# A one-core forward and backward pass of attention and SwiGLU: W' stored untransposed in the second MLP chunk and turned by its load, four q tiles stored earlier, and half of the MLP gradient loads moved to ScalarE's queue

## The chip, the core and the metric

One core of a Trainium2 chip. TensorE (PE) multiplies matrices; VectorE (DVE), ScalarE (ACT) and GpSimd (POOL) do the rest; SyncE (SP), ACT and POOL issue DMAs, which 16 DMA engines carry out. Each issuer has a queue of its own (q1 for SP, q10 for ACT and q0 for POOL in the profile). The metric is the device time of one launch, in microseconds (us), median of several runs.

## What is computed

```python
def _B_ref(x, w1, w3, w2):
    gate = x @ w1;  up = x @ w3
    return (silu(gate) * up) @ w2
def _A_ref(x, wqkv, wo):                    # 32 heads of 20
    q, k, v = heads(x @ wqkv)
    phi = lambda t: where(t > 0, t + 1, exp(t)) + 1e-6
    kv = einsum("hsd,hse->hde", phi(k), v);  z = phi(k).sum(s)
    num = phi(q) @ kv;  den = phi(q) @ z + 1e-6
    return heads_joined(num / den) @ wo
h  = x + _A_ref(layernorm(x), wqkv, wo)
h2 = h + _B_ref(layernorm(h), w1, w3, w2)
# outputs: h2 and, from grad_out, the gradients of x, wqkv, wo, w1, w3, w2
```

(Shortened: the einsums of the reference are written as products, and the reference takes the gradients by differentiation of this function.) S = 2048 rows, D = 640, F = 1728, all in bf16. Rows come in 16 tiles of 128 (t), and in four chunks of 512 (c); F in 13 pieces of 128 and one of 64 (fc); D in five pieces of 128.

## The kernel before

The program's order is written out by hand: each engine runs its instructions in the order in which the Python code records them, with semaphores where one needs another's result. A DMA's completion is a semaphore too. The stages:

1. *Phase 1, to about 75 us.* Layer norm, k, v and the first q tiles; kv is formed without v: the kernel keeps M = phi(k)^T x and applies W_v to it later. phi(q) of tile t, times 1/den, is called r; pqT holds it transposed. r is stored in DRAM as r_d for the backward pass.
2. *The prelude to the MLP, about 75 to 100 us*, the list in `run((...), ...)`. `q_late(t)` forms the last six q tiles; tiles 8 to 15 are not yet divided, and are kept in DRAM (pq_d, by `q_out` and `q_rest`) until `r_load` brings them back in the MLP. `f2_wT(i)` forms 128 rows of the transposed W', where W' = blockdiagonal(kv) wo, in the buffer pkx, and issues a DMA transpose on SP that writes 128 columns of Wp, W' itself. `f2_w_out` stores pkx's part, the transposed W', as wT_d. `f2_half(t, j)` multiplies r by half of Wp, adds x and takes the statistics of the second layer norm; `f2_hn(t)` normalises on DVE and stores hn_d; `f2_ht(t)` turns the tile (on PE with a copy on ACT for the first four, by DMA after them). `mlp_ghh(n)` is one piece of grad_out w2^T.
3. *The MLP, about 100 to 345 us*: for each chunk c and fc, `mlp(c, fc, ...)`. ACT takes sigmoids and copies of two PSUM results, `mlp_pair` has DVE work on two fc at a time, and the results are stored: hh_d by SP, two pieces of gg_d by POOL, where the gate buffer (two of a kind) is free again only when its store has landed. Between the matmuls of fc stand the second product of the chunk before (`o2_steps`), and the attention output and layer norm of the chunk after (`sides`). `r_steps[c]` adds r's work at given fc. At c = 3, fc = 9 wT2, the transposed W', is loaded on SP.
4. *Gradient of w2, 345 to 404 us*, from hh_d.
5. *The backward pass through the MLP's layer norm, 404 to 540 us*: for each tile t, `b_ghn(t)` multiplies a piece of gg_d, loaded by `load_gg(j, c0, c1)` for two tiles at a time into two buffers ggb, with the transposed w1 and w3. `ln_bwd` then gives g_h, the gradient of h; `b_gT(t)` turns it by a DMA transpose on ACT's queue; `b_gr(t)` multiplies it by wT2 two steps later. In the same steps, ACT's queue also turns wo and kvT_d (woT, kvN), 128 rows at a time.
6. *The gradients of wqkv, wo, x, w1 and w3, 540 to 824 us.*

Which queue a DMA stands in, and what stands before it there, is set by the place of its line in this order: `dma` and `dmaT` (a transpose) are SP's, `dmaG` is POOL's, `A.dma_start` and `A.dma_start_transpose` ACT's. An issuing engine waits at a DMA until the data that it needs is there, and all behind it waits too. POOL also takes the power -0.5 of the variances (L154) and some products (L352).

Of the kernel before, what the change touches and what calls it, by code (L numbers as in the profile page):

```python
# [9 lines left out]
P = 128  # L10
BF16 = mybir.dt.bfloat16
# [7 lines left out]
S, D, H, F = 2048, 640, 32, 1728  # L19
DH = D // H  # L20
ST, DT = S // P, D // P
FT, FP = 14, 1792
# [3 lines left out]
NG = 27  # L26
# [29 lines left out]
def kernel(  # L56
# [19 lines left out]
    V, A, T, G, SY = nc.vector, nc.scalar, nc.tensor, nc.gpsimd, nc.sync  # L76
    dma, dmaT, dmaG = SY.dma_start, SY.dma_start_transpose, G.dma_start

    def rows(ap):
        return ap.rearrange("(t p) d -> p t d", p=P)  # L80
# [9 lines left out]
    dram = ctx.enter_context(tc.tile_pool(name="dram", bufs=1, space=bass.MemoryType.DRAM))  # L90
# [2 lines left out]
    pk_d = dram.tile([S, D], BF16, name="pk_d")  # L93
    xn_d = dram.tile([S, D], BF16, name="xn_d")
    m_d = dram.tile([D, D], BF16, name="m_d")
    wT_d = dram.tile([D, D], BF16, name="wT_d")
    kvT_d = dram.tile([D, D], BF16, name="kvT_d")
    dwoT_d = dram.tile([D, D], BF16, name="dwoT_d")
    hn_d = dram.tile([S, D], BF16, name="hn_d")
# [30 lines left out]
    class Stats:  # L130
# [8 lines left out]
        def run(self, src, a, b):  # L139
            for t in range(a, b):  # L140
                for j in range(2):
                    self.part(src, t, j)

        def part(self, src, t, j, mid=None):
            if j == 0:
                self.st[t] = cp.tile([P, 2, 6], F32, name="st6", bufs=4)
            V.bn_stats(out=self.st[t][:, j, :], in_=src[:, t, j * HD:(j + 1) * HD])  # L147
            if j == 0:
                return
            V.bn_aggr(out=self.mv[:, t, :], in_=self.st.pop(t)[:])  # L150
            if mid is not None:
                mid()
            V.tensor_scalar(out=self.ve[:, t:t + 1], in0=self.mv[:, t, 1:2], scalar1=EPS_LN, scalar2=None, op0=ALU.add)
            G.tensor_tensor(out=self.rs[:, t:t + 1], in0=self.ve[:, t:t + 1], in1=mhalf[:, 0:1], op=ALU.pow)  # L154
# [29 lines left out]
    def load_x(a, b):  # L184
        dma(out=x_sb[:, a:b, :], in_=xS[:, a:b, :])
# [35 lines left out]
    def load_g2T(c):  # L221
        g2T[c] = U2.tile([P, DT, W], BF16, name="g2T", tag="g2T", bufs=2)
        dmaT(out=g2T[c][:], in_=goD[c * W:(c + 1) * W, :])
# [87 lines left out]
    pkx = []  # L311
# [332 lines left out]
    def f2_wT(i):  # L644

        acc = [ps.tile([P, 512], F32, name="wt", tag=("o2", "at")[i % 2], bufs=2) for _ in range(2)]
        for c, a, b, bank, off, first in SQ:
            T.matmul(acc[bank][:, off:off + (b - a) * DH], lhsT=wo[:, c, i * P:(i + 1) * P],
                     rhs=bd[:, c, a * DH:b * DH], start=first, stop=True, skip_group_check=True)
        for bank, (a, b) in enumerate(((0, SPLIT_D), (SPLIT_D, H))):  # L650
            (A.copy, V.tensor_copy)[bank](out=pkx[0][:, i, a * DH:b * DH], in_=acc[bank][:, 0:(b - a) * DH])
        dmaT(out=Wp[:, :, i * P:(i + 1) * P], in_=pkx[0][:, i, :])

    def f2_w_out():
        dmaG(out=rows(wT_d), in_=pkx[0][:, 0:DT, :])

    def f2_m_out():
        dmaG(out=m_v[:, 4, :], in_=mbs[:, 0, :])
# [97 lines left out]
    def drain(n):  # L756
        for _ in range(min(n, len(later))):
            later.pop(0)()
# [61 lines left out]
    Wp = U1.tile([P, DT, D], BF16, name="Wp", tag="MW")  # L820
    pkx.append(p1.tile([P, DT + 6, D], BF16, name="pkx", tag="pk"))
    def kv3():
        for m in (2, 3, 4):
            f2_kv(m)

    run((q_late, 10, f2_mT), (q_late, 11, kv3), (phi_rest,), (r_store, 4, 5), (r4_out,),
        (q_late, 12, lambda: (f2_wT(0), f2_wT(1))), (q_late, 13, lambda: (f2_wT(2), f2_wT(3))), (phi_rest,),
        (q_late, 14, lambda: f2_wT(4)), (load_x, 4, 8), (r_head, 5), (r_prod, 7), (r_store, 5, 6), (f2_m_out,),
        (f2_w_out,), (q_out, 8, 10), (q_out, 10, 14), (load_w2T, 8 * P, 10 * P), (mlp_ghh, 4), (q_late, 15),
        (sig_table,), (f2_half, 0, 0), (f2_half, 1, 0), (f2_half, 2, 0), (f2_half, 0, 1), (f2_half, 1, 1), (f2_hn, 0),  # L830
        (f2_half, 2, 1), (f2_hn, 1), (f2_half, 3, 0), (f2_half, 3, 1), (f2_ht, 0), (mlp_ghh, 5), (load_w2T, 10 * P, F),
        (f2_hn, 2), (f2_ht, 1), (mlp_ghh, 6), (r_red, 6), (f2_hn, 3), (f2_ht, 2), (r_inv, 6), (r_scale, 6), (r_T, 6),
        (f2_half, 4, 0), (mlp_ghh, 7), (f2_ht, 3), (f2_half, 4, 1), (r_red, 7), (r_inv, 7), (r_scale, 7), (r_T, 7),
        (r_store, 6, 8))
    p1.release()
    pa = pool("pa", "right")

# [25 lines left out]
    def r_end(t):  # L863
# [4 lines left out]
                13: ((xn_out, 3, dmaG),)},  # L868
               {0: ((r_den, 8),), 1: ((r_end, 8), (r_load, 11)), 2: ((r_den, 9),), 3: ((r_end, 9), (r_load, 12)),
                4: ((r_den, 10), (q_rest,)), 5: ((r_end, 10), (r_load, 13)), 6: ((r_den, 11),),  # L870
                7: ((r_end, 11), (r_load, 14)), 9: ((r_den, 12),), 10: ((r_end, 12), (r_load, 15))},
               {0: ((r_den, 13),), 1: ((r_end, 13),), 3: ((r_den, 14),), 4: ((r_end, 14),), 6: ((r_den, 15),),
                7: ((r_end, 15),)}, {}]
    for c in range(SC):
        hhT[c] = pa.tile([P, FT, W], BF16, name="hhT", bufs=2)
        o2 = o2_steps(c - 1) if c > 0 else None

        def run_side(pos, fc):
            if c + 1 < SC:
                for f, i in sorted(sides[c][pos].get(fc, ()), key=lambda x: (x[0] is f2_ht, x[1])):  # L880
                    f((c + 1) * TPC + i)

        for fc in range(FT):
            mlp(c, fc, lambda: run_side(0, fc))
            drain(1)
            if o2 and not (c == SC - 1 and fc == 5):
                next(o2, None)
            run_side(1, fc)
            drain(1)
            if (c, fc) in ((0, 12), (1, 5)):  # L890
                load_x(8 + 4 * c, 12 + 4 * c)
            if c == 0 and fc in (5, 7, 9, 11):
                a, b = {5: (0, 3), 7: (3, 6), 9: (6, 10), 11: (10, 13)}[fc]
                dma(out=w2[:, a:b, :], in_=B_w2[a * P:b * P, :].rearrange("(c p) n -> p c n", p=P))
                if fc == 11:
                    dma(out=w2[0:FL, FT - 1, :], in_=B_w2[(FT - 1) * P:F, :])
            for f, *t in r_steps[c].get(fc, ()):
                f(*t)
            if c == 2 and fc == 3:
                dmaG(out=rows(kvT_d), in_=bd[:])  # L900
            if fc == (6, 3, 3)[min(c, 2)] and c < SC - 1:
                load_g2T(c + 1)
            if c == SC - 1 and fc == 0:
                g2 = U1.tile([P, ST, D], BF16, name="g2", tag="Q")
                tail = U2.tile([P, DT, P], BF16, name="w13tail", tag="g2T", bufs=2)
            if c == SC - 1 and fc in (1, 2, 5, 6):
                i = (1, 2, 5, 6).index(fc)
                dma(out=g2[:, i * TPC:(i + 1) * TPC, :], in_=goS[:, i * TPC:(i + 1) * TPC, :])
            if c == SC - 1 and fc == 8:
                dma(out=tail[:, :, 0:FL], in_=B_w1[:, F - FL:F].rearrange("(c p) f -> p c f", p=P))  # L910
                dma(out=tail[:, :, FL:P], in_=B_w3[:, 0:P - FL].rearrange("(c p) f -> p c f", p=P))
            if c == SC - 1 and fc == 9:
                wT2 = U1.tile([P, DT, D], BF16, name="wT2", tag="MW")
                dma(out=wT2[:], in_=rows(wT_d))
    drain(1)
    next(o2, None)
    drain(1)
# [34 lines left out]

    ggb = {}

    def load_gg(j, c0, c1):
        if c0 == 0:
            ggb[j] = ba.tile([P, NG, 2 * P], BF16, name="ggb", bufs=2)
        dma(out=ggb[j][:, c0:c1, :],
            in_=gg_d[c0 * P:c1 * P, j * 2 * P:(j + 1) * 2 * P].rearrange("(c p) w -> p c w", p=P))

    def gw2_tail():
# [50 lines left out]
    def b_load(t):  # L1012
        hnb[t] = br.tile([P, D], BF16, name="hnb", bufs=3)
        dma(out=hnb[t][:], in_=hn_v[:, t, :])
        dma(out=r_sb[:, t, :], in_=r_v[:, t, :])
# [40 lines left out]
    def by_dma(t):  # L1056
        return t < ST - 2
# [79 lines left out]
    for t in range(ST):  # L1137
        g = b_ghn(t)

        def part():  # L1140
            next(g, None)

        u = t - 2
        if 2 <= t <= ST - 3:
            load_gg(t // 2 + 1, *((FT, NG) if t % 2 else (0, FT)))
        part()
        part()
        part()
        if t + 2 < ST:
            b_load(t + 2)  # L1150
        if t >= 1:
            ln_rest.pop(t - 1)()
            if by_dma(t - 1):
                b_gT(t - 1)
            if t <= 2 * DT:
                n = (t - 1) % DT
                dst, src = (woT, A_wo) if t <= DT else (kvN, kvT_d)
                A.dma_start_transpose(out=dst[:, :, n * P:(n + 1) * P], in_=src[n * P:(n + 1) * P, :])
        part()
        if u >= 0:  # L1160
            b_gr(u)
        part()
        part()
        if u >= 0:
            b_gq(u)

        if t >= 4:
            load_xn(t - 4, t - 3)
# [290 lines left out]
```

## Time and profile before

| | |
|---|---|
| median of 7 runs | 825.7 us (824.85 to 828.0) |
| the profiled execution | 826.12 us, its span 824.4 us |
| PE busy | 816.3 us, 99% of the span |
| DVE, ACT, POOL busy | 452.8, 319.9, 133.4 us |
| chain of work that ended last | PE 87%, DVE 6%, DMA 4%, issue 1%, ACT 1% |
| DMA, 60 to 120 us | the 16 engines taken 1.00 to 1.12 of the time, 225 to 263 GB/s |
| DMA over the span | 157.58 MB, mean 191 GB/s |

The page gives for each engine its busy time, and for a group of instructions its line, engine, operation, tiles (out<-in) and count. The waits view says who waited for whom: us in total, times, longest. The timeline shows merged instructions in order of time: start, duration, engine, line, operation; the idle time before them stands in brackets with what ended it. In the DMA list stand the issuer, the count, the KB of each and the median us from issue to landing. The trace also holds a record of each DMA packet: queue, start, duration, bytes. Matmuls overlap one another, so a busy PE says only that no gap was seen; the spacing of their starts says more.

### The profile page before, as it was taken

To read this page: it belongs to the slowest core of one execution; us is meant where nothing else is said; L and a number is where in the kernel's file an instruction comes from. 1 tells how busy PE (TensorE), PEld (TensorE's weight loads), DVE (VectorE), ACT (ScalarE), POOL (GpSimd) and SP (SyncE) were. 2 spreads that over 40 slices of the span, in tenths; PEclk is the share of its full clock that TensorE was granted. 3 is DMA by queue.
4 is the path that set the end of the run, shared out by engine and by line. 5 is a ranking of instruction groups with operands and counts; after the bars stand their busy time and mean duration, and the time that the engine had idled before them with its cause. 6 is when DMAs were issued, how large, how long until landed. Compare 5 with 4: busy or idle time off the path is not lost.

```text
span 824.4 us, 14215 instructions
## 1 busy us (share of the span) xinstructions
PE 816.3 (99%) x5549; PEld 522.5 (63%) x5549; DVE 452.8 (55%) x961; ACT 319.9 (39%) x607; POOL 133.4 (16%) x193
## 2 busy tenths in 40 slices
PE   8999999999999999999999999999999999999998
PEld 5677544555555555777777777777777777555554
DVE  7859987999898566300057777772681544200000
ACT  6856787655655666011121212222212334211111
POOL 2244433233322212100001111110220000000000
PEclk9999999999999999999999999999999999999999
DMA  9899999596494555999778899358994788985771
GB/s 242 227 313 224 217 266 293 194 236 172 126 225 127 153 184 167 228 249 262 211 166 182 197 215 197 59 110 179 279 189 108 164 196 183 210 199 128 174 160 38
DMA packets 318338, 157.58 MB, mean 191 GB/s; under 512 B 235456, under 2 KB 311456, under 8 KB 318272
## 3 DMA queue, kind: packets, MB, share of 16 engines
q1 hardware_dynamic: 286256, 120.65, 63.3%
q0 software_dynamic: 7376, 24.81, 9.5%
q10 hardware_dynamic: 24640, 11.23, 6.8%
q8 instruction: 43, 0.70, 0.4%
q14 instruction: 23, 0.19, 0.1%
HBM read 48.15 MB, written 51.46 MB: 121 GB/s over the span
## 4 chain that ended last, share of the span: by engine, by line
PE 87%; DVE 6%; DMA 4%; issue 1%; ACT 1%; POOL 0%; SPq 0%; DVEq 0%; ACTq 0%; POOLq 0%
PE job L1223 19%; PE mm L380 16%; PE ghn L1025 14%; PE gxn L1381 8%; PE o L791 7%; PE gw L980 7%; PE gwo L1110 3%; PE gr L1082 3%; PE dkv L1327 3%; DMA gg_d<-gate 2%; PE macc L411 2%; DVE st L147 2%; PE big L265 2%; PE at L610 1%; PE dkv L1255 1%
## 5 line engine op out<-in xcount | busy, mean ns | idle before, releaser
L1223 PE MATMUL job<-gb,hnN 128*128 128x432 bf16 (+2 forms) x656 | 117.0, 342 | 0.0
L1025 PEld LDWEIGHTS <-ggb 128*128 128x128 bf16 x864 | 84.5, 98 | 32.8
L1223 PEld LDWEIGHTS <-hnN 128*128 128x128 bf16 x656 | 63.6, 98 | 53.4
L380 PE MATMUL mm<-pqT,w 128*128 128x512 bf16 x405 | 93.6, 379 | 0.3 <-ACT pqT L703 0.3
L380 PEld LDWEIGHTS <-w 128*128 128x128 bf16 x540 | 52.5, 98 | 63.4 <-issue 1.3
L1227 ACT CAST obs<-job 128x432 bf16<-128x432 f32 (+3 forms) x61 | 29.3, 481 | 123.0 <-PE job L1223 123.0
L791 PE MATMUL o<-w,hhT 128*128 128x320 bf16 x448 | 67.5, 299 | 0.0
L1025 PE MATMUL ghn<-w13a,ggb 128*128 128x320 bf16 x448 | 63.5, 299 | 0.0
L1025 PE MATMUL ghn<-w13b,ggb 128*128 128x320 bf16 x416 | 61.4, 299 | 0.0
L380 PE MATMUL mm<-g2T,w2T 128*128 128x512 bf16 x240 | 59.6, 379 | 0.3 <-ACT gate L732 0.3
L791 PEld LDWEIGHTS <-hhT 128*128 128x128 bf16 x448 | 43.8, 98 | 23.6
L980 PE MATMUL gw<-g,hb 128*128 128x320 bf16 x416 | 56.8, 299 | 0.0
L1090 POOL TENSOR_TENSOR sz<-Zb,g_h 128x640 f32<-128x640 bf16 x16 | 20.2, 1262 | 199.3 <-DVE g_h L1088 199.3
L980 PEld LDWEIGHTS <-hb 128*128 128x128 bf16 x416 | 40.6, 98 | 16.0 <-issue 0.3
L1381 PE MATMUL gxn<-wqT,gT 128*128 128x320 bf16 x320 | 48.7, 299 | 0.0
L400 ACT CAST ghh<-mm 128x512 bf16<-128x512 f32 x48 | 28.3, 589 | 47.0 <-PE mm L380 41.5
L730 ACT ACTIVATE sig<-mm 128x512 bf16<-128x512 f32 x56 | 33.6, 600 | 26.5 <-PE mm L380 23.6
L265 PE MATMUL big<-wqkv,pqT 128*128 128x320 bf16 x260 | 40.0, 299 | 2.0 <-DMA wqkv<-in_A_wqkv_dram 1.0
L1037 ACT ACTIVATE gs<-ghn 128x640 bf16<-128x640 f32 x16 | 11.3, 704 | 79.0 <-PE ghn L1025 74.0
L380 PEld LDWEIGHTS <-w2T 128*128 128x128 bf16 x260 | 25.3, 98 | 23.8 <-issue 0.6
L265 PEld LDWEIGHTS <-pqT 128*128 128x128 bf16 x320 | 30.4, 98 | 15.3 <-issue 1.6
L1381 PEld LDWEIGHTS <-gT 128*128 128x128 bf16 x320 | 31.3, 98 | 12.2
(207 smaller groups left out, 1280.4 us busy)
## 6 DMA issues: line engine op xcount, KB each, us to landing
gg_d<-gate POOLq DMA_DIRECT2D x24, 256.0 KB, 4.0
hh_d<-hhT SPq DMA_DIRECT2D x24, 256.0 KB, 2.7
gg_d<-ghh POOLq DMA_DIRECT2D x24, 256.0 KB, 3.5
ggb<-gg_d SPq DMA_DIRECT2D x6, 896.0 KB, 5.6
ggb<-gg_d SPq DMA_DIRECT2D x6, 832.0 KB, 7.2
x_sb<-in_A_x_dram SPq DMA_DIRECT2D x7, 640.0 KB, 6.9
out_dram<-obs ACTq DMA_DIRECT2D x39, 108.0 KB, 3.0
ggb<-gg_d SPq DMA_DIRECT2D x2, 1728.0 KB, 12.6
```

Source lines behind the costliest of these rows:

```text
L265: T.matmul(acc, lhsT=pqT[:, c, t * P:(t + 1) * P], rhs=wqkv[:, c, n0:n0 + HD], start=(c == 0), stop=(c == DT - 1))
L380: T.matmul(acc[:], lhsT=w[:, c, fc * P:(fc + 1) * P], rhs=rhs[:, c, :], start=(c == 0), stop=(c == DT - 1))
L400: A.copy(out=ghh[n // 2][:, n % 2, :], in_=acc[:])
L730: A.activation(sig[:, i, :], gp[:], AF.Sigmoid)
L791: T.matmul(o2["ps"][:, 0:HD], lhsT=hhT[c][:, fc, i * P:(i + 1) * P], rhs=w2[:, fc, j * HD:(j + 1) * HD], start=(fc == 0), stop=(fc == FT - 1))
L980: T.matmul(acc[:, j, 0:HD], lhsT=hb[b][:, t, i * P:(i + 1) * P], rhs=g2[:, t, j * HD:(j + 1) * HD], start=(t == 0), stop=(t == ST - 1))
L1025: T.matmul(acc[:, j, 0:HD], lhsT=ggb[t // 2][:, k, lo:lo + P], rhs=rhs[:, j * HD:(j + 1) * HD], start=(k == 0), stop=(k == NG - 1))
L1082: T.matmul(gr[t][:, j, 0:HD], lhsT=ghT[t][:, c, :], rhs=wT2[:, c, j * HD:(j + 1) * HD], start=(c == 0), stop=(c == DT - 1))
L1110: T.matmul(acc[m][:, j, 0:n], lhsT=r_sb[:, t, m * P:(m + 1) * P], rhs=g_hx[:, t, j * HD:j * HD + n], start=(t == 0), stop=(t == ST - 1))
L1223: T.matmul(acc[:, 0:n], lhsT=lhs[:, t, m * P:(m + 1) * P], rhs=rhs(t), start=(t == 0), stop=(t == ST - 1))
L1227: A.copy(out=ob, in_=acc[:, 0:n])
L1381: T.matmul(acc[:, j, 0:HD], lhsT=g, rhs=wqT[:, k, j * HD:(j + 1) * HD], start=(k == 0), stop=(k == 14))
```

## The change

- `f2_w_out` is gone from the prelude. In its place `w_out` stores Wp, W' untransposed, as w_d on POOL's queue, in chunk 1 after fc = 11. wT2's load at c = 3, fc = 9 becomes a DMA transpose of w_d on SP.
- `q_out(8, 10)` and a new `q_out(10, 12)` stand before `q_late(12)`; `q_out(12, 14)` stays at the old place.
- `load_x(4, 8)` becomes `load_x(4, 6)` there, and `load_x(6, 8)` near the end of the list, between `f2_half(4, 1)` and `r_red(7)`.
- `f2_hn(2)` stands before `f2_half(3, 1)` instead of after `mlp_ghh(5)` and `load_w2T(10 P, F)`.
- In stage 5 the first half of a ggb load (14 of 27 pieces) stays on SP at the even step t. The second (13 pieces), which stood on SP at the head of the odd step, is issued by ACT in the even step, after g_h's transpose and that of wo or kvT_d. The number of loads and their bytes are the same.

```diff
-    wT_d = dram.tile([D, D], BF16, name="wT_d")
+    w_d = dram.tile([D, D], BF16, name="w_d")
...
-    def f2_w_out():
-        dmaG(out=rows(wT_d), in_=pkx[0][:, 0:DT, :])
+    def w_out():
+        dmaG(out=rows(w_d), in_=Wp[:])
...
-    run((q_late, 10, f2_mT), (q_late, 11, kv3), (phi_rest,), (r_store, 4, 5), (r4_out,),
-        (q_late, 12, lambda: (f2_wT(0), f2_wT(1))), (q_late, 13, lambda: (f2_wT(2), f2_wT(3))), (phi_rest,),
-        (q_late, 14, lambda: f2_wT(4)), (load_x, 4, 8), (r_head, 5), (r_prod, 7), (r_store, 5, 6), (f2_m_out,),
-        (f2_w_out,), (q_out, 8, 10), (q_out, 10, 14), (load_w2T, 8 * P, 10 * P), (mlp_ghh, 4), (q_late, 15),
-        (sig_table,), (f2_half, 0, 0), (f2_half, 1, 0), (f2_half, 2, 0), (f2_half, 0, 1), (f2_half, 1, 1), (f2_hn, 0),
-        (f2_half, 2, 1), (f2_hn, 1), (f2_half, 3, 0), (f2_half, 3, 1), (f2_ht, 0), (mlp_ghh, 5), (load_w2T, 10 * P, F),
-        (f2_hn, 2), (f2_ht, 1), (mlp_ghh, 6), (r_red, 6), (f2_hn, 3), (f2_ht, 2), (r_inv, 6), (r_scale, 6), (r_T, 6),
-        (f2_half, 4, 0), (mlp_ghh, 7), (f2_ht, 3), (f2_half, 4, 1), (r_red, 7), (r_inv, 7), (r_scale, 7), (r_T, 7),
-        (r_store, 6, 8))
+    run((q_late, 10, f2_mT), (q_late, 11, kv3), (phi_rest,), (r_store, 4, 5), (r4_out,), (q_out, 8, 10),
+        (q_out, 10, 12), (q_late, 12, lambda: (f2_wT(0), f2_wT(1))), (q_late, 13, lambda: (f2_wT(2), f2_wT(3))),
+        (phi_rest,), (q_late, 14, lambda: f2_wT(4)), (load_x, 4, 6), (r_head, 5), (r_prod, 7), (r_store, 5, 6),
+        (f2_m_out,), (q_out, 12, 14), (load_w2T, 8 * P, 10 * P), (mlp_ghh, 4), (q_late, 15), (sig_table,),
+        (f2_half, 0, 0), (f2_half, 1, 0), (f2_half, 2, 0), (f2_half, 0, 1), (f2_half, 1, 1), (f2_hn, 0),
+        (f2_half, 2, 1), (f2_hn, 1), (f2_half, 3, 0), (f2_hn, 2), (f2_half, 3, 1), (f2_ht, 0), (mlp_ghh, 5),
+        (load_w2T, 10 * P, F), (f2_ht, 1), (mlp_ghh, 6), (r_red, 6), (f2_hn, 3), (f2_ht, 2), (r_inv, 6), (r_scale, 6),
+        (r_T, 6), (f2_half, 4, 0), (mlp_ghh, 7), (f2_ht, 3), (f2_half, 4, 1), (load_x, 6, 8), (r_red, 7), (r_inv, 7),
+        (r_scale, 7), (r_T, 7), (r_store, 6, 8))
...
-                7: ((r_end, 11), (r_load, 14)), 9: ((r_den, 12),), 10: ((r_end, 12), (r_load, 15))},
+                7: ((r_end, 11), (r_load, 14)), 9: ((r_den, 12),), 10: ((r_end, 12), (r_load, 15)), 11: ((w_out,),)},
...
-                dma(out=wT2[:], in_=rows(wT_d))
+                dmaT(out=wT2[:], in_=w_d[:, :])
...
-    def load_gg(j, c0, c1):
+    def load_gg(j, c0, c1, q=dma):
         if c0 == 0:
             ggb[j] = ba.tile([P, NG, 2 * P], BF16, name="ggb", bufs=2)
-        dma(out=ggb[j][:, c0:c1, :],
+        q(out=ggb[j][:, c0:c1, :],
...
-        if 2 <= t <= ST - 3:
-            load_gg(t // 2 + 1, *((FT, NG) if t % 2 else (0, FT)))
+        ahead = 2 <= t <= ST - 4 and t % 2 == 0
+        if ahead:
+            load_gg(t // 2 + 1, 0, FT)
...
                 A.dma_start_transpose(out=dst[:, :, n * P:(n + 1) * P], in_=src[n * P:(n + 1) * P, :])
+            if ahead:
+                load_gg(t // 2 + 1, FT, NG, A.dma_start)
```

## The prediction

> **What bounds the kernel now.** I read the busy table first, then the waits of TensorE (PE), the chain, and then the four places that they name, engine by engine. The busy table:
>
> ```profile
> span 824.4 us, 14215 instructions
> ...
> PE 816.3 (99%) x5549; PEld 522.5 (63%) x5549; DVE 452.8 (55%) x961; ACT 319.9 (39%) x607; POOL 133.4 (16%) x193
> ```
>
> PE is busy for all but 8.1 us. PE's instruction order is the same in both kernels, so no PE work can be saved; the change can only shorten or lengthen PE's gaps. Asked for 75 to 345 us, all that lies between phase 1 and the weight gradients, the waits of PE are:
>
> ```profile
> PE mm L380 <- ACT pqT L703: 0.3, 1, 0.3
> PE mm L380 <- ACT gate L732: 0.3, 1, 0.3
> PE at L610 <- DMA Wp<-pkx: 0.2, 1, 0.2
> PE trh L702 <- DVE hn L160: 0.2, 1, 0.2
> ```
>
> Four waits, one each. From 404 to 540 us, where the gg pieces are loaded, PE has no wait. PE's timeline dates the four (us of start, us, tile; idle time in brackets):
>
> ```profile
> 87.59 2.20 PE L610 MATMUL at<-Wp,pqT 128*128 128x320 bf16 x15 [0.22 <-DMA Wp<-pkx]
> ...
> 96.74 0.45 PE L702 MATMUL trh<-ident,hn 128*128 128x128 bf16 x5 [0.21 <-DVE hn L160]
> ...
> 100.22 5.12 PE L380 MATMUL mm<-pqT,w 128*128 128x512 bf16 x23 [0.31 <-ACT pqT L703]
> ...
> 143.02 1.24 PE L380 MATMUL mm<-g2T,w2T 128*128 128x512 bf16 x5 [0.28 <-ACT gate L732]
> ```
>
> The brackets leave out the drain of the matmul before. From start to start, less the usual spacing (0.136 us for 320 columns, 0.216 for 512), the four cost 0.38, 0.37, 0.48 and 0.45: **1.68 us in all, 0.2% of the time. That is the most that this change can bring**; what it can cost has no such cap. 0.2%, 1.65 us, is also about what a measurement of this kernel can tell from no change.
>
> Where the first wait comes from stands in SyncE's (SP's) timeline, and in the DMA list (KB, us to landing):
>
> ```profile
> 78.71 0.54 SPq L185 DMA_DIRECT2D x_sb<-in_A_x_dram  x1
> 81.10 7.04 SPq L652 DMA_TRANSPOSE Wp<-pkx  x5
> ```
>
> ```profile
> wT_d<-pkx POOLq DMA_DIRECT2D x1, 800.0 KB, 13.1
> ...
> r_d<-pq POOLq DMA_DIRECT2D x1, 640.0 KB, 6.4
> pq_d<-pkx POOLq DMA_DIRECT2D x1, 640.0 KB, 13.2
> ```
>
> The five transposes that make Wp stand on SP's queue behind a 640 KB load of x. The first half of `f2_half(0)` needs the first three; the third landed at 87.46 and PE went on at 87.59. At the same time POOL's queue stores r_d. By the packet records it moves 5120-byte packets from 79.5 to 82.4 us (16 in each 0.25 us, some 320 GB/s), and x gets going only as it ends: 2 packets per 0.25 us at 81.5, 40 to 58 from 82.25 on.
>
> **What the Trainium skill says.** "DMA: Bandwidth & Descriptors", section "Issuing engines are not separate DMA queues": DMAs of different issuers run on the same 16 engines and interleave. Its section "Queues, rings and completion order": each engine goes round its queues packet by packet. The trace agrees, and shows the price: at 98 to 99 us, while wT_d and pq_d are stored, 13 to 18 POOL packets of 5120 bytes pass per 0.25 us and only 15 to 28 of SP's 256-byte transpose packets; alone, a transpose runs 265 to 285 per 0.25 us. A transpose beside a POOL store nearly stands still. Beside a plain load it is milder: at 92.0 to 92.75 us x still moved 32 to 62 packets of 1280 bytes per 0.25 us.
>
> **The change, part by part.** Against the profiled execution: 826.12 us, its span 824.4 and 1.7 around it; the median of the runs is 825.7, 0.4 less, so I add the sum to the median.
>
> *(a) Four late q tiles stored sooner.* `q_out(8,10)` and `q_out(10,12)` move in front of `q_late(12)`: two POOL issues of 0.76 us and 640 KB, 128 packets of 5120 bytes, right behind r_d. The second waits for DVE's pkx of tile 11 (done at 80.7). Behind them on POOL stands only `r_prod(7)`, which did not start before 85.8. So POOL's queue stays busy past 82.4 us, against the x load and the Wp transposes behind it. From below: x and the stores together moved some 416 GB/s at 92 to 93 us, against 280 for x alone at 82.5 to 84, so 602 KB of x left plus 655 KB end at 82.25 + 3.0 = 85.3 instead of 84.5: +0.8; with a part lost in the slow tail that x has anyway (84.75 to 85.25), +0.3. From above: 128 packets at 10 per 0.25 us are 3.2 us in which transposes crawl; at the undisturbed 16 they are 2.0. Less than nothing is excluded: nothing ahead of Wp is taken away. I take **+1.2 us (0.3 to 2.5)** on PE's wait at 87.6. The other two transposes keep their cover: the fifth landed at 89.80, PE needed it at 89.84, and PE comes later by the same delay.
>
> *(b) `f2_w_out` gone there, `load_x(4,8)` cut into (4,6) and (6,8), `q_out(12,14)` smaller.* 800 KB less in POOL's burst of 88 to 104 us, 640 KB gone to (a). SP's w2T transpose, which held SP for 10.3 us, gets through sooner, and so do r_T(5) (landed 104.2, wanted 108.9) and the hn_d stores. None of these ended a wait of PE: **0**. The second part of x is issued after r_T(6), near 108 us, and wanted at 118: hidden, with some 4 us left after a landing of 5 to 7 us.
>
> *(c) `f2_hn(2)` ahead of `f2_half(3,1)`.* DVE's timeline:
>
> ```profile
> 94.96 0.89 DVE L147 BATCH_NORM_STATS2 st<-x_sb 128x6 f32<-128x320 bf16 x2
> ...
> 96.24 0.45 DVE L160 TENSOR_SCALAR hn<-x_sb,ln_mv,ln_rs 128x640 bf16<-128x640 bf16 x1
> ```
>
> hn(2) now goes between the two statistics, some 0.8 us sooner; PE came for it 0.37 us too soon. The wait at 96.7 goes: **-0.37 (0 to -0.37)**. Next in line is hn(3), which POOL's power (0.73 us) and `r_red(6)` put at about the same place as before (97.8; PE wants it at 98.4). The wait at 100.2, `f2_ht(3)`'s copy on ACT, is an order of PE, ACT, PE that nothing here alters: it stays.
>
> *(d) The wait at 143.* gate's buffer waits for its store, issued 135.7, landed 142.3 beside an 819 KB load. Neither is touched, though their alignment shifts: **0 (-0.45 to +0.4)**.
>
> *(e) `w_out` in chunk 1 after fc 11.* An 800 KB store, 0.88 us on POOL at 202.2, behind the ghh store and ahead of gate's of 204.5. Its 160 packets take 2.5 us at 16 per 0.25, so POOL's queue is busy from 204.5 to 207 or 208. In it lies the last transpose of chunk 2's hnT: issued 202.97, landed 207.38, and PE takes it up at 208.68. Slack 1.3 us; I expect a landing of 208.2 to 209.9. **+0.2 (0 to 1.2)**. gate's store behind it had 2.4 us to spare before ACT's next write.
>
> *(f) Wp turned by wT2's load.* A transpose in place of a 0.55 us copy at 315.4: the same shape, dwoT_d at 708.9, held SP for 4.5 us and landed after 7.0. Behind it on SP comes a store that does not issue until 323.2; wT2 is read at 423. The gate store beside it (landed 321.4) has 2.8 us before its buffer is written. **0 (0 to 0.5)**.
>
> *(g) The second half of gg on ACT's queue, behind g_h's transpose.* Six loads of 832 KB move from SP to ACT, some 0.4 us of issue each, after woT's or kvN's transpose. In every second step that transpose now lands in 3 us instead of 7 (2.6 to 7.2 in the trace); gr had about 1.6 us to spare (447.66 landed, 449.23 begun), so PE gains nothing. Behind the load on ACT is gs of the same step, due 2.7 us after the first transpose's end, with 1.3 to 2.6 us of woT's before it: it may slip by 0.5 us, inside that slack and two ghn accumulators. gg is read a step later: **0**.
>
> Sum: 1.2 - 0.37 + 0 + 0.2 = **+1.0**; as the high tail of (a) has its own case below, I put the likeliest at +0.8: **826.5 us**.
>
> **Rivals.**
> *Slower: the q stores starve Wp.* Transposes stop for the whole burst, as at 98 us; PE waits 2.0 to 3.2 us more at 87.6, less 0.37, plus 0.2: about +2.4, 828.1. It decides from a delay of 2.0 us on. For it: the 98 us packets; against it: x, a plain load, stands first in SP's queue and shares well. Chance 0.30.
> *Slower: W' lands on the chunk boundary.* (e) at its upper end or beyond, 1.2 us on top of 1.2 - 0.37: +2.0, 827.7. Against it: 1.3 us of slack. Chance 0.10.
> *Faster.* (a) is absorbed by x's tail, the shorter burst at 88 to 104 also lets chunk 0's stores land sooner, and three or four of the waits go: -1.3 to -1.68, with a little luck of the runs 824.0. Chance 0.12.
> *The likeliest*, +0.8, within 0.2%: 0.48; its own range is 824.6 to 827.3 (from 0.3 - 0.37 - 0.45 to +1.6, and half a us of scatter downward).
>
> **How the numbers follow.** Faster by over 0.2%: 0.12; within: 0.48; slower: 0.30 + 0.10 = 0.40. The range takes in the starved case and most of the fast one: 824.2 to 828.6.
>
> **What would show it.** (a): r_d and pq_d packets up to 85 us, x_sb later than 85.5, PE's bracket at `at<-Wp` near 1.4 us instead of 0.22. (c): no wait of trh on hn. (e): a wait of mm L380 on DMA pqT near 208 us. (f), (g): PE still free of waits from 404 to 540, ghT's landings all under 5 us. I am wrong if the bracket at 87.6 has not grown, or if a wait appears that stands in none of (a) to (g).

## The result, and the profile after

The changed kernel takes **830.68 us** (median of 12 runs, 828.54 to 832.65) against 826.08 for the kernel before in the same comparison (31 runs). The ratio is 1.0054, 95% interval 1.0045 to 1.0064: **slower by 4.5 us** (4.6 by the medians). The prediction was +0.8, with a range that ended at 828.6.

The profiled execution took 830.10 us. Its span has grown by 4.0 us, and PE's busy time hardly:

```profile
span 828.4 us, 14228 instructions
...
PE 817.4 (99%) x5549; PEld 523.2 (63%) x5549; DVE 453.3 (55%) x961; ACT 320.2 (39%) x607; POOL 133.8 (16%) x194
```

So the loss is in PE's gaps. The waits of PE from 75 to 345 us, as in the prediction (us in total, times, longest):

```profile
PE at L610 <- DMA Wp<-pkx: 4.1, 2, 2.8
PE mm L380 <- DMA pqT<-hn: 1.1, 1, 1.1
PE mm L380 <- ACT pqT L703: 0.3, 1, 0.3
```

Two of the four old waits are gone, hn and gate; Wp has grown from 0.2 to 4.1 and is now two waits; one is new. PE's timeline shows the two, and that the larger is the second:

```profile
88.61 2.20 PE L610 MATMUL at<-Wp,pqT 128*128 128x320 bf16 x15 [1.36 <-DMA Wp<-pkx]
90.64 0.30 PE L608 MATMUL at<-x_sb,ident 128*128 128x320 bf16 x1
93.70 0.85 PE L610 MATMUL at<-Wp,pqT 128*128 128x320 bf16 x5 [2.75 <-DMA Wp<-pkx]
```

The first group reads W's first 320 columns, which need the third transpose; the second group needs the fifth. From start to start, less the usual spacing, as in the prediction:

| PE's wait, us | before | after |
|---|---|---|
| third Wp transpose | 0.38 | 1.53 |
| fifth Wp transpose | 0.08 | **2.92** |
| hn | 0.37 | 0 |
| ACT pqT | 0.48 | 0.48 |
| 140 to 155 us | 0.45 | 0.19 |
| hnT of chunk 2, 212 us | 0 | **1.29** |
| sum | 1.76 | 6.41 |

The sum grows by 4.65 us, the span by 4.0. The difference lies outside this stretch: the kv matmuls at 77.28 us began 0.13 us sooner, and 0.51 us less passed after the last matmul.

*Where the fifth transpose lost its time.* SP's timeline of after:

```profile
78.69 0.53 SPq L185 DMA_DIRECT2D x_sb<-in_A_x_dram  x1
80.95 8.98 SPq L652 DMA_TRANSPOSE Wp<-pkx  x5
```

From the first issue to the end of the fifth 8.98 us passed instead of 7.04: the second alone held SP for 2.99 us instead of 1.3, so the fifth went out at 88.53 and not at 86.94. POOL's timeline (DMA issues; the bracket says what POOL waited for):

```profile
78.28 0.71 POOL L672 DMA_DIRECT2D pq_d<-pq  x1 [0.31 <-DVE bd L210]
80.83 0.72 POOL L672 DMA_DIRECT2D pq_d<-pkx  x1 [1.84 <-DVE pkx L641]
...
88.19 0.59 POOL L679 DMA_DIRECT2D r_d<-pql  x1 [0.98 <-DVE pql L366]
88.78 0.55 POOL L658 DMA_DIRECT2D m_d<-mbs  x1
89.33 0.71 POOL L672 DMA_DIRECT2D pq_d<-pkx  x1
```

These last three lines are POOL's second burst. It begins where it did before (at 88.19; before at 88.33). The fifth transpose used to be out 1.4 us ahead of it; now it is out 0.34 us behind. By the packet records 592 of the transpose's 640 packets of 256 bytes had ended by 91.0 us. The last 48 took until 92.05 (0.3 us in the kernel before), and 32 packets of 4 bytes that close it until 93.20; between 91.0 and 93.5 us POOL had 94 of its 5120-byte packets end. It landed at 93.65 (before: 89.80), as the burst ran out (m_d at 93.36, pq_d at 94.15). From 91.0 to 92.0 almost nothing ended on either queue, one packet of POOL's and 44 of the transpose's; POOL's packets begun at 91 took up to 1.07 us each. What they waited for, no run here shows.

*The first wait* is the prediction's step (a). The early q stores kept POOL's packets going up to 83.3 us and again from 84.4 to 86.2. x reached its full rate at 83.0 (before 82.25), yet landed only 0.22 us later (85.72, before 85.50). The transposes behind it lost more: by 85.25 us 35 of their packets had ended, against 494 in the kernel before. The third landed at 88.47 (before 87.46).

*The third loss* shows in the chain of waits (start, us, what):

```profile
206.20 6.74 DMA pqT<-hn
213.19 2.32 PE mm L380 x10
```

`w_out`, issued at 205.41, moved some 17 packets of 5120 bytes per 0.25 us from 208.5 to 210.0, and its last ones by 211.96. Beside it the last of the transposes of chunk 2's hn got 3 to 12 packets of 256 bytes per 0.25 us until 210.5; it took 6.74 us instead of 4.4.

### The profile page after: what moved, and what is told of

Same layout as the page of the kernel before. It is cut to its first block, busy times and chain, and to the rows that moved or that the text cites. A ratio compares the mean times of both kernels' runs of the same rounds, so it can differ in the third digit from the quotient of the medians.

```text
span 828.4 us, 14228 instructions
## 1 busy us (share of the span) xinstructions
PE 817.4 (99%) x5549; PEld 523.2 (63%) x5549; DVE 453.3 (55%) x961; ACT 320.2 (39%) x607; POOL 133.8 (16%) x194
## 4 chain that ended last, share of the span: by engine, by line
PE 92%; DVE 4%; DMA 2%; ACT 1%; issue 1%; SPq 0%; POOL 0%; DVEq 0%; ACTq 0%
PE job L1226 19%; PE mm L380 19%; PE ghn L1025 14%; PE gxn L1384 8%; PE gw L980 7%; PE o L791 7%; PE gwo L1110 3%; PE gr L1082 3%; PE dkv L1330 3%; PE macc L411 2%; PE at L610 2%; PE big L265 2%; DVE st L147 1%; PE mm L265 1%; DMA pqT<-hn 1%; DMA Wp<-pkx 1%
```

## The experiments

All were timed beside the kernel before, whose median was 825.84 to 825.97 in the four sessions. "Ratio" is the time over that of the kernel before, with its 95% interval in parentheses. A wait "from start to start" is measured as in the prediction, and is a little longer than the figure in a list of waits.

### Which part of the change costs: e1 to e4

**e1**, the kernel before with the early q stores alone:

```diff
-    ... (r_store, 4, 5), (r4_out,),
+    ... (r_store, 4, 5), (r4_out,), (q_out, 8, 10), (q_out, 10, 12),
...
-        (f2_w_out,), (q_out, 8, 10), (q_out, 10, 14), ...
+        (f2_w_out,), (q_out, 12, 14), ...
```

> The kernel before, with only the two q stores of tiles 8 to 11 moved in front of q_late(12). Theory: these 640 KB on GpSimd's queue hold up x and the Wp transposes behind it, and cost both waits of f2_half on Wp (1.53 and 2.92 us from start to start in the kernel after, against 0.38 and 0.08 before): about +4.0 us, ratio 1.004 to 1.006, with the fifth Wp transpose issued after 88 us and landed after 92. Rival: the waits come of the changes together (the smaller load of x, the moved hn, the shorter second burst); then this kernel is within 1 us of the kernel before and the waits on Wp stay under 0.6 us each.

Measured: 830.31 us (5 runs), ratio 1.0044 (1.0027 to 1.0061). PE's waits:

```profile
PE at L610 <- DMA Wp<-pkx: 2.7, 2, 2.1
PE mm L380 <- ACT pqT L703: 0.3, 1, 0.3
PE trh L702 <- DVE hn L160: 0.2, 1, 0.2
```

This edit alone brings nearly the whole loss. It falls otherwise on the two waits than expected: from start to start they are 2.27 us on the third transpose and 0.95 on the fifth. The fifth was issued at 88.52, again behind the burst (88.07), and landed at 93.48; PE came for it later than in the kernel after, so it waited less. In this execution nine matmuls between the two ran at half clock (see the last section).

**e2**, the reverse: the kernel after, with the q stores back at their old place.

```diff
-    ... (r4_out,), (q_out, 8, 10), (q_out, 10, 12), (q_late, 12, ...
+    ... (r4_out,), (q_late, 12, ...
...
-        (f2_m_out,), (q_out, 12, 14), ...
+        (f2_m_out,), (q_out, 8, 10), (q_out, 10, 14), ...
```

> The kernel after, with only the two q stores put back to their old place behind f2_m_out. Theory: both waits on Wp return to under 0.5 us and 4.0 us come back; the wait on the chunk boundary (1.29 us, the transpose of hn behind the store of W') stays, the wait on hn (0.37) stays away: 826.1 + 1.3 - 0.4, less up to 0.45 at 143 us, so 826.5 to 827.0, ratio 1.0005 to 1.0015. Rival: the waits have another cause in the change; then it stays near 830.7.

Measured: 826.55 us (13 runs), ratio 1.0009 (0.9996 to 1.0023). Waits of PE:

```profile
PE mm L380 <- DMA pqT<-hn: 1.2, 1, 1.2
PE at L610 <- DMA Wp<-pkx: 0.3, 1, 0.3
...
```

Some 4 us come back. What is left above the kernel before is the boundary wait, 1.41 us from start to start, while hn and gate no longer cost anything.

**e3**, the kernel before with only gg's second half on ACT's queue, and **e4**, the kernel before with only `f2_hn(2)` moved:

```diff
+            if ahead:
+                load_gg(t // 2 + 1, FT, NG, A.dma_start)      # e3
...
-        ... (f2_half, 3, 0), (f2_half, 3, 1), ... (f2_hn, 2), (f2_ht, 1),
+        ... (f2_half, 3, 0), (f2_hn, 2), (f2_half, 3, 1), ... (f2_ht, 1),   # e4
```

> The kernel before, with only the second half of the gg loads moved to ScalarE's queue. Theory: nothing, 826.1 within 0.4 us; no wait of PE from 404 to 540 us in either, g_h's transposes landed within 5 us of issue at the most, instead of 7.2. Rival: ScalarE's gs comes late behind the loads; then the same +0.5 us or more in each second step, and waits of PE there.

> The kernel before, with only f2_hn(2) moved ahead of f2_half(3,1). Theory: the wait of trh on hn (0.37 us from start to start) goes and nothing takes its place: 825.7, ratio 0.9995. Rival: hn(3) or ScalarE's copy of the fourth tile is late by the same; then the same time as before, and the wait before mm L380 at 100 us grows by 0.3 to 0.4.

Measured: e3 825.75 us (21 runs), ratio 0.9990 (0.9982 to 0.9998); e4 825.54 (14 runs), ratio 0.9991 (0.9978 to 1.0005). Both are at the edge of what can be measured: e3's interval just leaves out 1, e4's does not. In e3 PE has no wait from 404 to 540, and ghT lands within 4.6 us (before: 7.2). In e4 the wait for hn is gone and none takes its place. e4, and e7 below, which keep the old gg loads, show PE 0.28 and 0.44 us late at one matmul on ghT each, from start to start; in e4 a transpose landed after 8.8 us. Before and e1, with the old loads too, show no such wait, and none of the profiles with the moved loads does. So the move of gg to ACT seems to remove a wait that comes in some executions only; one profile of each kernel does not prove it.

### The boundary: e5

The kernel of e2, with `w_out` moved from chunk 1, fc 11 to chunk 3, fc 3:

```diff
-                7: ..., 9: ((r_den, 12),), 10: (...), 11: ((w_out,),)},
+                7: ..., 9: ((r_den, 12),), 10: (...)},
...
-                7: ((r_end, 15),)}, {}]
+                7: ((r_end, 15),)}, {3: ((w_out,),)}]
```

> The kernel after, with the q stores back at their old place and w_out moved from chunk 1, fc 11 to chunk 3, fc 3, where no hnT transpose is on SP's queue any more. Theory (the 800 KB store starves the last transpose of chunk 2's hnT): the 1.41 us wait of mm L380 on DMA pqT near 207 us, which the kernel with only the q stores put back has, goes below 0.1; the time falls by about 1.3 us from that kernel's 826.55 to 825.0-825.4, ratio to before 0.998-0.9995; wT2, loaded at fc 9, still lands long before gr needs it. Rival (the transpose is late because SP's queue itself issues later, by the altered alignment of the stores): the wait stays above 0.8 us and the ratio at 1.000-1.001.

Measured: **824.96 us** (22 runs), ratio 0.9985 (0.9975 to 0.9994). Waits of PE:

```profile
PE at L610 <- DMA Wp<-pkx: 0.4, 1, 0.4
PE mm L380 <- ACT pqT L703: 0.3, 1, 0.3
```

The boundary wait is gone with the store, and 1.6 us of the time, as the theory said: the store did delay the transpose, which now landed after 5.26 us, against 6.87 in e2. This is also the best version found, 1.0 us under the kernel before and 5.7 under the kernel after by their medians.

### How the q stores reach the fifth transpose: e6 to e8

**e6**, the kernel after, with POOL's second burst behind `f2_hn(1)`:

```diff
-        ... (r_prod, 7), (r_store, 5, 6), (f2_m_out,), (q_out, 12, 14), ...
+        ... (r_prod, 7), ...
...
-        (f2_half, 2, 1), (f2_hn, 1),
+        (f2_half, 2, 1), (f2_hn, 1), (r_store, 5, 6), (f2_m_out,), (q_out, 12, 14),
```

> The kernel after, with POOL's second burst (r_store(5,6), f2_m_out, q_out(12,14)) moved behind f2_hn(1), so that it is issued some 7 us later; the early q stores and w_out stay where after has them. Theory (two collisions: the q stores hold up x and the first transposes, then the second burst meets the fifth transpose, which is late by then): the wait on the third Wp transpose stays near 1.5 us, the one on the fifth falls from 2.9 us to 0-0.8; no half clock; the boundary wait of 1.3 us stays; time 827.0-828.2, ratio 1.0015-1.0030. Rival (the fifth is late only because SP issues it late, 88.5 instead of 86.9): it lands near 91-93 all the same, its wait stays above 1.8 us and the ratio at 1.004 or more. Unknown: what the later burst does to hn's stores and the transposes behind them; up to +1.

Measured: 827.88 us (22 runs), ratio 1.0013 (1.0001 to 1.0025). Waits of PE:

```profile
PE at L610 <- DMA Wp<-pkx: 2.3, 1, 2.3
PE mm L380 <- DMA pqT<-hn: 1.4, 1, 1.4
PE mm L380 <- ACT gate L732: 0.7, 1, 0.7
...
```

The fifth transpose, issued late again (87.96), lands in 2.78 us and is waited for no more. So its delay came from the second burst, not from the late issue by itself; the late issue only moved it into the burst. The wait on the third stays (2.46 us from start to start in this execution, against 1.53 in the kernel after), and so does the one at the boundary.

**e7**, the kernel before with only `q_out(8, 10)` early, half the bytes:

```diff
-    ... (r_store, 4, 5), (r4_out,),
+    ... (r_store, 4, 5), (r4_out,), (q_out, 8, 10),
```

> The kernel before, with q_out(8,10) alone moved early (320 KB); q_out(10,14) stays. Theory (the delay grows with the bytes put ahead, and jumps when the fifth transpose is pushed into POOL's second burst): half the bytes give a first wait of 0.8-1.4 us and a fifth transpose that lands by 91.5, so a wait there under 1 us; time +0.6 to +2.0, ratio 1.001-1.0025. Rival (it is q_out(10,12), stored 84.5-85.5 straight across the Wp transposes, that does the harm): the waits stay at 0.4-0.6 in all and the ratio is 1.000 within 0.001.

Measured: 827.28 us (22 runs), ratio 1.0019 (1.0006 to 1.0032). The waits are 1.02 us on the third and 0.88 on the fifth, which landed at 90.45. Half the bytes, about a third of the loss: the harm is not in the second store alone.

**e8**, the opposite of the change: the kernel of e5 with `r_store(4, 5)` and `r4_out` too taken from ahead of x and put at the head of the second burst:

```diff
-    ... (phi_rest,), (r_store, 4, 5), (r4_out,),
+    ... (phi_rest,),
...
-        (r_prod, 7), (r_store, 5, 6), ...
+        (r_prod, 7), (r_store, 4, 5), (r4_out,), (r_store, 5, 6), ...
```

> The kernel of this call with w_out at chunk 3, and in addition r_store(4,5) and r4_out (640 KB and 160 KB of r_d) taken from their place before q_late(12) to the head of POOL's second burst. The opposite of the change: nothing of POOL's stands ahead of x and the Wp transposes. Theory: x lands 1.5-2.5 us sooner (near 83.5), the third Wp transpose by 86, the waits at Wp (0.3-0.5 us) vanish; 824.6-825.0, 0.3-0.5 us under the other one. Rival: the second burst, now 1.3 MB, begins at the same place but lasts 3 us longer and starves w2T, hn's stores or r_T(5): a new wait of 0.5-2 us of mlp_ghh on w2T or of f2_half on pqT, and no gain or a loss.

Measured: 825.75 us (22 runs), ratio 0.9990 (0.9979 to 1.0001), 0.8 us above e5. x landed at 82.34, the first four transposes 2.6 us after their issue each, and the wait on the third is gone. But the burst now began at 87.21, right behind the fifth's issue at 86.66, which took 3.80 us:

```profile
PE at L610 <- DMA Wp<-pkx: 1.0, 1, 1.0
...
```

The wait had moved from the third transpose to the fifth (1.19 us from start to start). My theory foresaw the first half of this and missed the second, the same mistake as in the prediction.

How far the burst's first issue stood behind that of the fifth transpose, and how long the transpose took, in all the profiles (e9 to e12 are described below):

| kernel | burst behind, us | fifth, issue to landing, us |
|---|---|---|
| before, e2 to e5 | 1.16 to 1.51 | 2.83 to 2.87 |
| e8 | 0.55 | 3.80 |
| e7 | 0.44 | 3.34 |
| e9 | -0.16 | 5.42 |
| after | -0.34 | 5.13 |
| e1 | -0.45 | 4.95 |
| e6, e10 to e12 | burst moved behind its landing | 2.57 to 2.78 |

### The burst behind the layer norm: e10, e11, e12

Can the burst go behind the fifth transpose altogether? In **e10** all of e8's burst stands behind `f2_hn(0)`; in **e11** e5's second burst alone; in **e12** e8's burst is cut in three, behind `f2_hn(0)`, `f2_hn(2)` and `f2_hn(3)`.

```diff
-        (r_prod, 7), (r_store, 4, 5), (r4_out,), (r_store, 5, 6), (f2_m_out,), (q_out, 8, 10), (q_out, 10, 14), ...
+        (r_prod, 7), ...
...
-        ... (f2_half, 1, 1), (f2_hn, 0),
+        ... (f2_half, 1, 1), (f2_hn, 0), (r_store, 4, 5), (r4_out,), (r_store, 5, 6), (f2_m_out,), (q_out, 8, 10), (q_out, 10, 14),
```

e11's burst, from e5, and e12's, from e8:

```diff
+        ... (f2_hn, 0), (r_store, 5, 6), (f2_m_out,), (q_out, 8, 10), (q_out, 10, 14),                        # e11
...
+        ... (f2_hn, 0), (r4_out,), ... (f2_hn, 2), (r_store, 4, 5), (r_store, 5, 6), (f2_m_out,), ...         # e12
+        (f2_hn, 3), (q_out, 8, 10), (q_out, 10, 14), ...                                                     # e12
```

> The kernel with r_store(4,5) and r4_out late, and w_out at chunk 3, with the whole of POOL's burst (r_store(4,5), r4_out, r_store(5,6), f2_m_out, q_out(8,10), q_out(10,14), 1.4 MB) moved on behind f2_hn(0), so that it is issued after the fifth Wp transpose has landed. Theory (each Wp transpose is late only when a POOL store is under way beside it): all five land 2.6-2.8 us after their issue, no wait of PE on Wp at all, instead of 1.03 us on the fifth; 824.2-824.9 if nothing else comes up, ratio 0.9975-0.9992. Rival: the burst, now 94 to 104 us, starves hn's stores, w2T or r_T(5), and chunk 0's gate stores stand behind it on POOL: a new wait of 0.5-1.5 us of mlp_ghh on w2T or of mm on gate, and 825-826.

> The kernel with w_out at chunk 3 and the q stores at their old place, with POOL's second burst alone (r_store(5,6), f2_m_out, q_out(8,10), q_out(10,14)) moved behind f2_hn(0); r_store(4,5) and r4_out stay early. Theory: the fifth transpose is clear of POOL, but it already was (2.84 us to landing); the 0.6 us wait on the third, from r4_out ahead of x, stays; time within 0.3 us of 825.0. Rival as above: a new wait behind the later burst, 825.5-826.

> The kernel with w_out at chunk 3 and all of POOL's stores late, with the burst cut in three so that POOL never holds up the layer norm's power for long: r4_out behind f2_hn(0) (0.76 us of issue), r_store(4,5), r_store(5,6) and f2_m_out behind f2_hn(2) (1.7 us), q_out(8,10) and q_out(10,14) behind f2_hn(3) (1.5 us). Theory (the 2.2 us wait for hn came from 4 us of DMA issues on POOL ahead of hn(2)'s power, nothing else): no wait of PE on Wp and less than 0.4 us on hn; 824.2-825.0 unless the stores, which now end near 107 us, come into the way of the MLP's first buffers, which lie on the memory that pq and pkx leave. Rival (that, or hn(3) and the transposes of hn beside the stores): a new wait of 1 us or more between 98 and 115 us, 825.5-827.

Measured: e10 827.82 us (21 runs), ratio 1.0022 (1.0015 to 1.0030); e11 826.19 (13 runs), 0.9999 (0.9991 to 1.0008); e12 829.25 (6 runs), 1.0039 (1.0025 to 1.0053). All three are slower than was expected of them. In none of the three is a wait for Wp listed (from start to start at most 0.2 us are left): with the burst out of the way, Wp is in time. But PE waits for hn instead, 2.37 us in e10, 1.10 in e11 and 3.02 in e12 from start to start. DVE's waits tell why, e10 first and then e12:

```profile
DVE hn L160 <- POOL ln_rs L154: 2.8, 1, 2.8
```

```profile
DVE hn L160 <- DMA r_d<-pql: 3.4, 1, 3.4
```

In e10 POOL's six issues, 3.9 us, stood ahead of hn(2)'s power on POOL; e11, with four, had the same wait for 1.5 us. In e12 they no longer did, and the next thing was late: hn(2) lies in one of the four buffers pql, which is free only when r_d's store of the tile in it has landed. My expectation of e12 took the power for the only reason and was wrong. Of the places tried for the second burst, that of the kernel before is the best.

### Filling PE's pauses: e9

The kernel after, with 15 matmuls of 512 columns whose result nobody reads, 5 ahead of `f2_half(0, 0)` and 10 ahead of `f2_half(0, 1)`. It was to show whether the half clock of TensorE, described at the end, comes from these pauses.

```diff
+    def filler(n):
+        ...
+        for _ in range(n):
+            T.matmul(fl[0][:], lhsT=ident[:], rhs=pqT[:, 0, 0:512], start=True, stop=True)
...
-        (f2_half, 0, 0), (f2_half, 1, 0), (f2_half, 2, 0), (f2_half, 0, 1), ...
+        (filler, 5), (f2_half, 0, 0), (f2_half, 1, 0), (f2_half, 2, 0), (filler, 10), (f2_half, 0, 1), ...
```

> The kernel after, with 15 matmuls of 512 columns whose result nobody reads: 5 ahead of f2_half(0,0) and 10 ahead of f2_half(0,1), where PE waits 1.5 and 2.9 us for Wp. At the spacing of 0.216 us they take 1.1 and 2.2 us, nearly all of it inside the waits. Theory (a pause of PE of 2 to 3 us is what halves the granted clock for 3.4 us in some of the runs): with PE busy through the pauses, no run shows a mean clock of 0.998 or less, all lie between 828.3 and 831, and the median falls from 830.7 to 829.2-830.0 although work was added. Rival (the half clock comes from something else, and goes with the time of the run only by chance): two runs in five still show 0.998 or less and lie at 831.5 or more, median 830.5 or above.

Measured: 833.11 us (6 runs), ratio 1.0078 (1.0056 to 1.0100); two of the six runs had a mean granted clock of 0.998. None had been expected, and a time of 829.2 to 830.0. The experiment settles nothing: the two pauses at Wp shrank to 0.56 and 0.78 us, by 3.1 us in all, but the added matmuls took 3.2, the boundary wait, which I had left in, was 2.48 us here, and a gap of 1.6 us on DVE's g_k came up at 625 us, whose cause I did not follow.

## Why the prediction was wrong, step by step

- **(a), first half: the size right, in part by luck.** The wait on the third transpose grew by 1.15 us; the step took 1.2. The bracket of 1.36 is close to the 1.4 that was named, and POOL's packets up to 85 us came as foreseen. But the sum behind it was of x, which landed only 0.22 us later; the rest the transposes lost beside POOL's packets. And the size is that of one execution: in e1 and e6, with the same early stores, the wait grew by 1.89 and 2.08 us. (Two rates in the sum were read a little off: by the packet records x and the stores moved some 400 GB/s at 92 to 93 us, not 416, and x some 300 at 82.5 to 84, not 280. That would make its +0.8 a +1.1.)
- **(a), second half: this step failed.** It says "The other two transposes keep their cover: the fifth landed at 89.80, PE needed it at 89.84, and PE comes later by the same delay". The fifth does come later, and PE too; but POOL's second burst does not move with them, because it waits for DVE's pql, as its bracket says, and not for Wp. The step's list of what stands behind the q stores on POOL ended at `r_prod(7)`; the burst is what comes next. The cover was 1.4 us between the fifth's issue (86.94) and the burst (88.33), not 0.04 us at PE. A delay of 1.6 us put the transpose behind the burst: **+2.84 us, costed at nothing**. e1 shows that it belongs to the q stores, e6 that the second burst does it, and the table under e8 how the landing follows the lead.
- **The slower rival** had the mechanism (transposes starve beside POOL's stores) but named the first burst alone; there the loss was 1.15 us in this profile, below the 2.0 from which it would decide, though e6 shows 2.08 at the same place. The larger part came from the second burst. By the Trainium skill, "DMA: Bandwidth & Descriptors", section "Queues, rings and completion order", an engine goes round its queues by the packet. The trace of after agrees in part: from 92.0 to 93.25 us 90 of POOL's large packets end and 75 of SP's, of 4 to 1280 bytes, but from 208.5 to 210.5 it is 126 against 65. I had cited that for the first burst and did not ask it of the second, though the 98 us example was drawn from that burst.
- **(c): right.** The wait for hn is gone, -0.37, and nothing took its place (e4).
- **(d):** -0.26 here, inside its bounds; the wait near 143 us differs from execution to execution (0.2 us in e4 and 0.9 in e6).
- **(e): right mechanism, wrong size.** The slack of 1.3 us was used up and 1.29 more (e2: 1.41), where the step allowed 0 to 1.2 and took 0.2. The landing came at the end of the window that I had given, 212.94 against 209.9 plus the 3.2 us by which all was late. I took only 0.2 us of wait, though this was again a 256-byte transpose beside POOL's 5120-byte packets. e5 shows the store to be the cause.
- **(b), (f), (g): right**, at nothing: no wait in the lists of after and e2 belongs to them. That the old gg loads cost 0.3 to 0.6 us in some executions (e4, e7) was not foreseen.

Sum of the steps as measured: 1.15 + 2.84 - 0.37 - 0.26 + 1.29 = +4.65, instead of +1.0; the term that stood at nothing is 2.84 of the 3.65 us that are missing.

## What to carry to other kernels

When a transfer is delayed, don't ask only whether its consumer is delayed as much: list what else is issued by other queues around its new place, and which of it hangs on something else and stays where it is. Here the fifth Wp transpose, of 256-byte packets, landed 2.6 to 2.9 us after its issue when the burst of 5120-byte packets was issued over a microsecond behind it or later, and 3.3 to 5.4 us after it otherwise. So look for such a store between the issue and the landing of a transpose that PE waits for, and put it where no transpose is due (here chunk 3 instead of the chunk boundary). An edit bundle is best taken apart: two of these edits gained a little at most, two lost, and the kernel with `w_out` at another place and the q stores back beat both kernels.

## What the runs showed of the hardware

**A clock window in which PE pauses for part of it can halve the clock of the next.** The granted clock is the share of TensorE's full clock that the trace lists. In e1 it is 0.5 from 90.02 us, for 3.413 us, after PE's pause of 2.27 us. The Trainium skill, "TensorE: Matmul & The Clock Gate", section "What's actually happening", speaks of a free-running window of 3413 ns and of half rate after an idle window. The grid agrees: in e1 the full clock before it lasts 85.333 us, 25.0 such windows. But the window need not be idle. Busy times by window, e1 first (start and end, length, PE busy and instructions, then the other engines; granted clock; DMA share and GB/s):

```profile
86.61:90.02 3.41, 1.31 (x10) 0.75 (x9) 1.13 (x2) 2.80 (x6) 2.43 (x4) 1.00 0.99 211
90.02:93.44 3.42, 2.89 (x12) 1.32 (x9) 2.69 (x6) 0.00 (x0) 0.81 (x2) 0.50 1.06 254
```

and e6, whose pause of 2.46 us is the longer one but lies across two windows:

```profile
87.06:90.47 3.41, 1.45 (x11) 1.10 (x12) 0.86 (x3) 1.96 (x4) 0.00 (x0) 1.00 0.90 181
90.47:93.89 3.42, 3.42 (x27) 2.45 (x26) 3.28 (x9) 1.04 (x3) 0.23 (x1) 1.00 1.18 186
```

PE busy for 1.31 of 3.41 us: halved. Busy for 1.45: not. e10 (1.20 busy) and e12 (0.56) were halved too. In no other window of these 14 traces, from 8 us to the end of PE's work, was PE busy for less than 1.7 us, and none of them was followed by half clock. So on these traces the bound lies between 1.31 and 1.45 us of work, some 40% of a window, and whether a given pause crosses it depends on where the grid lies in that execution. Of the kernel after, five of the 12 runs had a mean clock of 0.998, one half window, and took 831.6 to 832.7 us; the seven at 1.000 took 828.5 to 831.3. A half window can cost at most 1.7 us, so it is a part of that difference and not all of it; which pause set it off in those runs was not traced.

**One DMA transpose issue can hold its queue for more than twice its time.** The second Wp transpose held SP for 2.99 us in after, 2.37 in e1 and 2.53 in e6, while x's load and POOL's stores were still under way. It took 1.3 in before, and 1.21 in e10, where no store of POOL's stood beside it. That is how 640 KB on POOL's queue delayed SP's issues behind it.
